# Loading the key weights in two transfers beside a second queue, with products of zeros ahead of the first folds

## The chip, the core and the metric

The kernel runs on one core of a Trainium2 chip. The core has five engines, each with its own instruction stream: TensorE (matrix products, PE in the profile, with its weight loads as PEld), VectorE (DVE), ScalarE (ACT), GpSimd (POOL) and SyncE (SP). SyncE only issues transfers here; SPq in the profile is its queue of issues. The engines wait for one another and for transfers by semaphores. The metric is the device time of one execution in microseconds (us); a run is told by its median over several executions. Beside the times there is one profiled execution, whose span runs from the first instruction to the last.

## What is computed

One block with a residual, over a sequence of 2048 positions with 512 channels. The input is layer-normalized; one branch is linear attention with a learned feature map, the other a gated two-layer network with a ReLU gate, whose output goes through SiLU and multiplies the attention's output.

```python
xn = layernorm(x)                                   # x: 2048 x 512
q, k, v = split(xn @ wqkv)                          # 32 heads of 16
pq, pk = q @ w_phi[h], k @ w_phi[h]                 # 16 x 16 per head
phi_q = concat(softmax(pq), softmax(-pq))
phi_k = concat(softmax(pk), softmax(-pk))
kv, z = phi_k.T @ v, sum(phi_k)
s = (phi_q @ kv / (phi_q @ z + 1e-6)) @ wo
gate, up = xn @ W_gate, xn @ W_up                   # 512 x 1376
g = silu(((gate * (gate > 0)) * up) @ W_down)
return x + s * g
```

All inputs and outputs are 32-bit floats.

## The kernel before

**Precision.** A 32-bit operand of a product is split into a high part, rounded to a format that TensorE multiplies in one pass (`F32R`), and a low part, the remainder. `split` (line 183) does this with one activation on ScalarE for the high part and one subtraction, on VectorE unless said otherwise, for the low part. `mm3` (line 188) then makes three products for each slice of 128 channels: low by high, high by low, high by high. So a projection of one tile of 128 positions is 12 products.

**The fold.** The feature map's weights `w_phi` are multiplied into the key and query weights once, at the start: `fold` (line 226) makes one slice of 128 rows of the combined weights by four plain 32-bit products of the raw weights (`wk_raw`, `wq_raw`, loaded transposed) with a block-diagonal constant `bd_sb` (tile `cb` in the profile, built on the host from `w_phi`). It returns a function that splits the result. There are four slices for keys and four for queries. Value weights are split without a fold (`wv_split`, line 852), with their low parts on GpSimd.

**The stages.** The 16 tiles of positions are normalized, transposed on TensorE by a product with an identity (`transpose_x`, line 277), split (`hi_xt`, `lo_xt`, lines 292 and 300, written to the tile `XT`), projected to keys, values and queries and turned into features; sums of key features with values are gathered in PSUM. Meanwhile the weights of the gated network are prepared. Then come two halves of that network with the queries' part of the attention beside it, and the output projection.

**Order.** The order of instructions on each engine is the order of the program's text (`InOrder`, line 39, keeps it), apart from work that a planner (`Clock`, line 56) inserts by estimated costs when it is pumped; the planner works while the program is built, with its own cost figures. An engine works through its instructions in order, and an instruction that waits holds back those behind it on its engine. On-chip buffers come from pools: `u2` has 44 buffers of 2 KB per partition, PSUM has 8 banks. Transfers from SyncE and ScalarE share eight semaphores in turn, so an issue waits until the transfer eight before it has landed.

**The start.** Lines 829 to 886 are the start of the program. SyncE issues x of the first tile, the block constants, the four slices of the key weights with the identity after the first slice, the second tile of x, halves of the query and value weights, and further tiles of x. `load_x` (line 213) issues one tile. VectorE computes the first tile's statistics and normalizes it (`norm_vector`, `norm_vector_apply`, lines 258 and 268), with GpSimd making the power of -1/2. TensorE's order is: folds of key slices 0 and 1, four transposes of the first tile (`turn`, line 304), folds of key slices 2 and 3, the 12 products of the first key projection (`pk`), folds of query slices 0 and 1, transposes of the second tile, folds of query slices 2 and 3, value projection (`pv`). The splits and `lo_xt` are in VectorE's order as the text has them: before the change the split of key slice 1 stands ahead of `lo_xt` of the first tile:

```python
    folds = [fold(WK, wk_raw[:, k, :], k) for k in range(2)]
    norm_vector_apply(0)
    folds[0]()
    px = turn(0, False)
    folds[1]()
    folds = [fold(WK, wk_raw[:, k, :], k) for k in range(2, KD)]
    lo_xt(*px)
    folds[0]()
    norm_vector(1)
    folds[1]()
    norm_vector_apply(1)
    pk = project(0, WK, "pk")
```

Nearly all instructions are recorded by one helper, so that the profile gives line 52 for them; tiles' names tell them apart: `pfold` is a fold's result, `pxT` a transposed tile, `wkh` and `wkl` the high and low part of a folded key slice, `wqh`, `wql` those of queries, `wvh`, `wvl` those of values, `xt` a tile of x, `xn` the normalized one.

Of the kernel before, what the change touches and what calls it, by code (L numbers as in the profile page):

```python
# [13 lines left out]
P = 128  # L14
# [5 lines left out]
KD = D // P  # L20
# [128 lines left out]
def layer_kernel(ctx: ExitStack, tc: tile.TileContext, x, wkT, wqT, wv, wo, wf, cst, out):  # L149
    pace = Clock()  # L150
    nc = InOrder(tc, pace)
# [4 lines left out]
    def ps(shape=(P, 512), name="ps"):  # L156
        return pp.tile(list(shape), F32, tag="ps", name=name)

    def u8(shape, name, dt=F32):
        return sb.tile(list(shape), dt, tag="u8", bufs=B8, name=name)  # L160
# [4 lines left out]
    def u2(shape, name, dt=F32):  # L165
        return sb.tile(list(shape), dt, tag="u2", bufs=B2, name=name)
# [7 lines left out]
    def f32(t):  # L174
        return t.bitcast(F32)

    def add(engine, o, a, b, op=ALU.add):
        engine.tensor_tensor(o, a, b, op=op)
# [31 lines left out]
    N = len(order)  # L210
    X = {}

    def load_x(n):
        b, i = order[n]
        t = b * TPB + i
        X[n] = u2((P, D), "xt")
        nc.sync.dma_start(X[n], x[t * P:(t + 1) * P, :])


    def w_tile(name):  # L220
# [5 lines left out]
    def fold(w, raw, k):  # L226

        p = ps(name="pfold")
        for j in range(KD):
            nc.tensor.matmul(p[:, j * P:(j + 1) * P], raw[:, j * P:(j + 1) * P], bd_sb[:, j, :],  # L230
                             start=True, stop=True)
        return lambda: split(*w[k], p)
# [44 lines left out]
    def transpose_x(n):  # L277
        p = ps((P, 2, 2, P), name="pxT")
        xn = XN.pop(n)
        for k in range(KD):  # L280
            transpose(p[:, k // 2, k % 2, :], xn[:, k * P:(k + 1) * P])
        return p

    def xt_parts(n, s):

        if n % 2 == 0:
            return [(XT[:, A11:A12 + 1, s, :, cols(n)], slice(0, 2))]
        if n not in A21:
            A21[n] = u2((P, 2, 2, P), "a21", F32R)
        return [(A21[n][:, s], 0), (XT[:, A22, s, :, cols(n)], 1)]  # L290

    def hi_xt(n, p):
        for to, c in xt_parts(n, 0):
            nc.scalar.activation(to, p[:, c], AF.Copy)

    def full_xt(n, p):
        XF[n] = u2((P, 2, 2, P), "xf")
        nc.scalar.activation(XF[n], p, AF.Copy)

    def lo_xt(n, p):  # L300
        for (to, c), (hi, _) in zip(xt_parts(n, 1), xt_parts(n, 0)):
            add(nc.vector, to, p[:, c], f32(hi), ALU.subtract)

    def turn(m, full=True):
        p = transpose_x(m)
        hi_xt(m, p)
        if full:
            full_xt(m, p)
        return m, p
# [519 lines left out]
    wk_raw, wv_raw, wq_raw = u8((P, KD, D), "wkT"), u8((P, KD, D), "wvr"), u8((P, KD, D), "wqT")  # L829
    bd_sb = u2((P, KD, P), "cb")  # L830
    ident = sb.tile([P, P], F32, name="ident")
    load_x(0)
    nc.sync.dma_start(bd_sb, cst[:, :KD, :])
    for k in range(KD):
        nc.sync.dma_start(wk_raw[:, k, :], wkT[:, k, :])
        if k == 0:
            nc.sync.dma_start(ident, cst[:, KD, :])
    load_x(1)
    nc.sync.dma_start(wq_raw[:, 0:2, :], wqT[:, 0:2, :])
    nc.sync.dma_start(wv_raw[:, 0:2, :], wv[:, 0:2, :])  # L840
    nc.sync.dma_start(wq_raw[:, 2:4, :], wqT[:, 2:4, :])
    load_x(2)
    nc.sync.dma_start(wv_raw[:, 2:4, :], wv[:, 2:4, :])
    for n in range(3, 7):
        load_x(n)
    mhalf = sb.tile([P, 1], F32, name="mhalf")
    nc.vector.memset(mhalf, -0.5)
    zacc = u4((P, H, 2, DH), "zacc")
# [7 lines left out]
    norm_vector_apply(0)  # L856
    folds[0]()
    px = turn(0, False)
    folds[1]()
    folds = [fold(WK, wk_raw[:, k, :], k) for k in range(2, KD)]  # L860
    lo_xt(*px)
    folds[0]()
    norm_vector(1)
    folds[1]()
# [9 lines left out]
    px = turn(1)  # L874
# [288 lines left out]
```

## Time and profile before

| what | value |
|---|---|
| median of 3 executions | 585.73 us (585.71 to 586.2) |
| profiled execution, its own time | 586.47 us |
| its span | 584.7 us |
| TensorE busy | 572.5 us (98%) |
| VectorE, ScalarE, GpSimd busy | 395.4, 288.6, 390.2 us |
| moved by transfers | 138.26 MB, 236 GB/s on average |

The span is shorter than the execution's own time by what lies around the first and last instruction. Rows of a timeline give the start in us from the span's start, the duration, the engine, the line, the operation, the tile written, the tiles read and how many instructions were merged; in brackets stands the idle time of the engine before it and what ended it. Rows of transfers give the size and the time from issue to landing. A plain 32-bit product of 128 by 128 with 128 columns appears as two instructions, here called passes.

### The profile page before, as it was taken

The numbers are of one execution on the slowest core, as the hardware profiler recorded it, in microseconds if no ns is written. First come the engines' busy times: TensorE is split into PE (matmuls) and PEld (weight loads), VectorE is DVE, ScalarE is ACT, GpSimd is POOL, SyncE is SP. The second block draws the span as 40 slices with busy tenths as digits, with TensorE's granted clock in tenths as the row PEclk, the third lists the DMA queues.
The fourth block names the chain that finished last, engine by engine and source line by source line (L and its number), as shares of the span: only waits on it lengthen the run. The fifth ranks groups of instructions, "written<-read, shape, count | busy, mean of one in ns | idle before, by whom it ended". The sixth has DMA issues, their size and how long they took to land.

```text
span 584.7 us, 8483 instructions
## 1 busy us (share of the span) xinstructions
PE 572.5 (98%) x2764; PEld 478.0 (82%) x2764; DVE 395.4 (68%) x604; ACT 288.6 (49%) x529; POOL 390.2 (67%) x341
## 2 busy tenths in 40 slices
PE   4999999999999999999999999999999999999997
PEld 4788888888888888888888888888888888888886
DVE  2898765876647976787784532488788868673323
ACT  3798786864635356245434151153554545534510
POOL 0669987998866576997967342544457585775394
PEclk9999999999999999999999999999999999999999
DMA  8358897974698938978967999995576475669863
GB/s 289 112 150 223 221 307 233 265 222 126 164 279 272 347 95 261 301 263 293 283 215 226 319 389 398 315 390 193 130 266 170 137 227 169 183 206 275 254 176 113
DMA packets 82844, 138.26 MB, mean 236 GB/s; under 512 B 7664, under 2 KB 30576, under 8 KB 81904
## 3 DMA queue, kind: packets, MB, share of 16 engines
q1 hardware_dynamic: 79488, 125.66, 64.3%
q0 software_dynamic: 3312, 12.06, 10.8%
q8 instruction: 22, 0.36, 0.3%
q14 instruction: 22, 0.18, 0.1%
HBM read 77.14 MB, written 52.69 MB: 222 GB/s over the span
## 4 chain that ended last, share of the span: by engine, by line
PE 97%; DMA 1%; ACT 1%; DVE 1%; SPq 0%; issue 0%; POOL 0%; POOLq 0%
PE py L52 21%; PE pd L52 10%; PE pa L52 10%; PE pc L52 10%; PE pso L52 8%; PE pk L52 8%; PE pq L52 7%; PE pv L52 7%; PE pb L52 5%; PE pkv L52 3%; PE pnum L52 3%; PE ppT L52 2%; PE pxT L52 1%; PE pfold L52 1%; DMA wkT<-wkT 1%; PE pkb L52 0%
## 5 line engine op out<-in xcount | busy, mean ns | idle before, releaser
L52 PE MATMUL pa<-XT,wa 128*128 128x512 f32 x264 | 68.9, 393 | 0.0
L52 PE MATMUL py<-fdh,hl 128*128 128x512 f32 x176 | 68.8, 391 | 0.0
L52 PE MATMUL py<-fdh,hh 128*128 128x512 f32 x176 | 68.6, 390 | 0.0
L52 PE MATMUL py<-fdl,hh 128*128 128x512 f32 x176 | 68.5, 389 | 0.0
L52 POOL TENSOR_TENSOR hl<-e,hh 128x512 fp32r<-128x512 f32 x22 | 28.4, 1292 | 56.5 <-ACT hh L52 56.2
L52 PEld LDWEIGHTS pa<-XT,wa 128*128 128x128 f32 x264 | 48.5, 188 | 9.4
L52 ACT ACTIVATE hh<-e 128x512 fp32r<-128x512 f32 x22 | 13.9, 632 | 72.1 <-DVE e L52 67.4
L52 POOL TENSOR_TENSOR phl<-ek,phl 128x1024 fp32r<-128x1024 f32 x15 | 36.1, 2403 | 17.9 <-ACT phl L52 17.9
L52 POOL TENSOR_TENSOR hl<-u,hh 128x512 fp32r<-128x512 f32 x22 | 28.5, 1296 | 27.1 <-ACT hh L52 24.8
L52 DVE TENSOR_TENSOR y<-py,y 128x512 f32<-128x512 f32 x40 | 27.5, 689 | 27.2 <-PE py L52 27.1
L52 POOL TENSOR_TENSOR y<-y,ys 128x512 f32<-128x512 f32 x24 | 31.1, 1297 | 17.0 <-ACT ys L52 17.0
L52 PEld LDWEIGHTS py<-fdh,hh 128*128 128x128 f32 x176 | 33.0, 188 | 7.0
L52 PEld LDWEIGHTS py<-fdl,hh 128*128 128x128 f32 x176 | 33.0, 188 | 6.7
L52 PEld LDWEIGHTS py<-fdh,hl 128*128 128x128 f32 x176 | 33.1, 188 | 6.7
L52 POOL TENSOR_TENSOR ez<-eq,zB 128x1024 f32<-128x1024 f32 x16 | 38.4, 2405 | 0.0
L52 DVE TENSOR_TENSOR pTl<-ppT,pTh 128x512 fp32r<-128x512 f32 x32 | 22.1, 690 | 23.1 <-ACT pTh L52 22.7
L52 PE MATMUL pd<-XT,wd 128*128 128x512 f32 x132 | 34.9, 395 | 0.0
L52 PE MATMUL pd<-XT,wc 128*128 128x512 f32 x132 | 34.5, 392 | 0.0
L52 PE MATMUL pb<-XT,wb 128*128 128x512 f32 x132 | 34.5, 393 | 0.0
L52 PE MATMUL pc<-XT,wb 128*128 128x512 f32 x132 | 34.3, 391 | 0.0
L52 POOL TENSOR_TENSOR ol<-of,oh 128x1024 fp32r<-128x1024 f32 x8 | 19.4, 2431 | 22.2 <-ACT oh L52 15.3
L52 PE MATMUL pc<-XT,wc 128*128 128x512 f32 x132 | 34.1, 391 | 0.0
(163 smaller groups left out, 1632.8 us busy)
## 6 DMA issues: line engine op xcount, KB each, us to landing
zacc<-ek POOLq DMA_DIRECT2D x15, 512.0 KB, 5.2
xts<-XT SPq DMA_DIRECT2D x4, 1792.0 KB, 11.3
XT<-xts SPq DMA_DIRECT2D x7, 1024.0 KB, 15.8
wa<-ws SPq DMA_DIRECT2D x26, 256.0 KB, 5.3
wb<-ws SPq DMA_DIRECT2D x26, 256.0 KB, 5.3
wc<-ws SPq DMA_DIRECT2D x26, 256.0 KB, 4.9
rawg<-wf SPq DMA_DIRECT2D x22, 256.0 KB, 3.9
ws<-wa SPq DMA_DIRECT2D x22, 256.0 KB, 3.9
```

Of the source, the lines that this page charges most:

```text
L52: return self.tc.keep_in_program_order(op(*a, **k))
```

## The change

The first tile of x, the block constants and the identity are issued by ScalarE, in this order, instead of SyncE. SyncE issues the key weights as two transfers of two slices each (512 KB), instead of four of 256 KB, and then goes on with the second tile of x and the other weights as before. A tile `idle` of 128 by 128 is set to zero by VectorE, and TensorE multiplies it with itself nine times into a PSUM tile that nothing reads. In the order of the program's text, `lo_xt` of the first tile now stands ahead of the split of key slice 1.

```diff
-    def load_x(n):
+    def load_x(n, queue=nc.sync):
         b, i = order[n]
         t = b * TPB + i
         X[n] = u2((P, D), "xt")
-        nc.sync.dma_start(X[n], x[t * P:(t + 1) * P, :])
+        queue.dma_start(X[n], x[t * P:(t + 1) * P, :])
...
-    load_x(0)
-    nc.sync.dma_start(bd_sb, cst[:, :KD, :])
-    for k in range(KD):
-        nc.sync.dma_start(wk_raw[:, k, :], wkT[:, k, :])
-        if k == 0:
-            nc.sync.dma_start(ident, cst[:, KD, :])
+    load_x(0, nc.scalar)
+    for k in (0, 2):
+        nc.sync.dma_start(wk_raw[:, k:k + 2, :], wkT[:, k:k + 2, :])
+    nc.scalar.dma_start(bd_sb, cst[:, :KD, :])
+    nc.scalar.dma_start(ident, cst[:, KD, :])
     load_x(1)
...
     for n in range(3, 7):
         load_x(n)
+
+    idle = u2((P, P), "idle")
+    nc.vector.memset(idle, 0.0)
+    p = ps((P, P), name="pidle")
+    for _ in range(9):
+        nc.tensor.matmul(p, idle, idle, start=True, stop=True)
     mhalf = sb.tile([P, 1], F32, name="mhalf")
...
     px = turn(0, False)
+    lo_xt(*px)
     folds[1]()
     folds = [fold(WK, wk_raw[:, k, :], k) for k in range(2, KD)]
-    lo_xt(*px)
     folds[0]()
```

## The prediction

> **What bounds the kernel now.** The page comes first: its span, its slices and the chain that ended last.
>
> ```profile
> span 584.7 us, 8483 instructions
> ...
> PE   4999999999999999999999999999999999999997
> ...
> PE 97%; DMA 1%; ACT 1%; DVE 1%; SPq 0%; issue 0%; POOL 0%; POOLq 0%
> ```
>
> TensorE is the bound: full in every slice but the first and the last, and 97% of the chain. Time can be had only where TensorE stands still, or runs slowly. The second view is the list of waits for TensorE over the whole run (us in total, times, longest).
>
> ```profile
> PE pfold L52 <- DMA wkT<-wkT: 7.1, 1, 7.1
> PE pk L52 <- DVE XT L52: 0.8, 1, 0.8
> PE pv L52 <- POOL wvl L52: 0.5, 2, 0.3
> PE pxT L52 <- DVE lr L52: 0.2, 1, 0.2
> ```
>
> The change touches the first two rows alone: 7.1 us until the key weights have landed, and 0.8 us before the first key projection. After them TensorE has almost no idle time, so what is won here reaches the end of the run unless a later wait takes it back. The third view is the timeline of the start (start and duration in us; SPq is SyncE's queue of issues).
>
> ```profile
> 0.75 1.28 ACT L52 ACT_TABLE_LOAD   x1 [0.75 <-PEq L1155]
> 0.75 0.38 SPq L52 DMA_DIRECT2D xt<-x  x1
> 0.82 0.06 DVE L52 MEMSET mhalf<- 128x1 f32 x1 [0.82 <-PEq L1155]
> 1.18 0.42 SPq L52 DMA_DIRECT2D cb<-cst  x1
> 1.65 0.42 SPq L52 DMA_DIRECT2D wkT<-wkT  x1
> ...
> 2.60 1.38 SPq L52 DMA_DIRECT2D wkT<-wkT  x3
> 3.49 0.69 DVE L52 BATCH_NORM_STATS2 bs<-xt 128x6 f32<-128x512 f32 x1 [2.61 <-DMA xt<-x]
> ...
> 4.49 0.43 SPq L52 DMA_DIRECT2D wqT<-wqT  x1
> ...
> 4.97 0.58 SPq L52 DMA_DIRECT2D wvr<-wv  x1
> 5.26 0.55 DVE L52 TENSOR_SCALAR xn<-xt,bm,br 128x512 f32<-128x512 f32 x1 [0.68 <-POOL br L52]
> ...
> 7.06 3.75 PE L52 MATMUL pfold<-cb,wkT 128*128 128x128 f32 x16 [7.06 <-DMA wkT<-wkT]
> ...
> 10.60 1.05 PE L52 MATMUL pxT<-ident,xn 128*128 128x128 f32 x4
> ...
> 11.46 1.99 PE L52 MATMUL pfold<-cb,wkT 128*128 128x128 f32 x16
> 11.70 0.60 ACT L52 ACTIVATE XT<-pxT 128x512 fp32r<-128x512 f32 x1 [1.96 <-PE pxT L52]
> ...
> 12.81 0.69 DVE L52 TENSOR_TENSOR wkl<-pfold,wkh 128x512 fp32r<-128x512 f32 x1 [2.35 <-ACT wkh L52]
> 13.42 0.68 DVE L52 TENSOR_TENSOR XT<-pxT,XT 128x512 fp32r<-128x512 f32 x1
> ...
> 14.02 0.68 DVE L52 TENSOR_TENSOR wkl<-pfold,wkh 128x512 fp32r<-128x512 f32 x1
> ...
> 14.25 0.47 PE L52 MATMUL pk<-wkh,XT 128*128 128x512 f32 x1 [0.81 <-DVE XT L52]
> ...
> 14.62 0.69 DVE L52 BATCH_NORM_STATS2 bs<-xt 128x6 f32<-128x512 f32 x1
> ...
> 15.62 0.68 DVE L52 TENSOR_TENSOR wkl<-pfold,wkh 128x512 fp32r<-128x512 f32 x1
> ...
> 16.64 0.39 PE L52 MATMUL pk<-wkl,XT 128*128 128x512 f32 x1
> ...
> 17.10 1.95 PE L52 MATMUL pfold<-cb,wqT 128*128 128x128 f32 x16
> ...
> 18.88 0.60 PE L52 MATMUL pxT<-ident,xn 128*128 128x128 f32 x4
> ...
> 19.32 1.95 PE L52 MATMUL pfold<-cb,wqT 128*128 128x128 f32 x16
> ```
>
> A fold of two key tiles is 16 passes. From the start of one group to the next, the first such pair takes 10.60 - 7.06 = 3.54 us, the same shape later 18.88 - 17.10 = 1.78 us; four transposes take 11.46 - 10.60 = 0.86 us at first and 19.32 - 18.88 = 0.44 us later. So TensorE runs at half rate from its first instruction until about 11.46, 4.40 us later.
>
> The fourth view is that of the transfers, one issue at a time (KB each, us from issue to landing), with the rate of the first 32 us in slices of 0.8 us.
>
> ```profile
> GB/s 0 0 113 379 256 145 250 231 243 289 333 417 422 425 407 425 397 422 397 392 389 361 254 18 0 20 0 0 0 0 0 0 0 133 195 0 0 0 54 338
> ...
> xt<-x SPq DMA_DIRECT2D x1, 256.0 KB, 2.7
> cb<-cst SPq DMA_DIRECT2D x1, 256.0 KB, 2.9
> wkT<-wkT SPq DMA_DIRECT2D x1, 256.0 KB, 5.3
> wkT<-wkT SPq DMA_DIRECT2D x1, 256.0 KB, 5.2
> wkT<-wkT SPq DMA_DIRECT2D x1, 256.0 KB, 6.2
> wqT<-wqT SPq DMA_DIRECT2D x1, 512.0 KB, 7.2
> wvr<-wv SPq DMA_DIRECT2D x1, 512.0 KB, 8.0
> ```
>
> With the issues above, x lands at 3.45, the constants at 4.08, the first key tile at 6.95, the second at 7.80, the fourth (issued near 3.55) at 9.75. While the key tiles move, in rows of 2 KB, the rate falls to 145 to 250 GB/s. The half query and half value weights, 512 KB in rows of 4 KB, land at 11.69 and 12.97, 1.28 us apart (410 GB/s).
>
> **The change part by part.** *Transfers.* SyncE issues two key transfers of 512 KB, in 4 KB rows, at once; ScalarE issues x, the block constants and the identity, at about 0.43 us each, and then loads its table (1.28 us), done near 0.75 + 1.3 + 1.28 = 3.3, long before its first activation. The first fold now waits for the constants and for both first key tiles. Were bytes alike whatever their order, x, constants and two key tiles would still land at 7.80, and the fold start near 7.9: that is the late end. If 4 KB rows move at the 410 GB/s of the query and value halves and the two queues share equally, 512 KB of keys are added to what landed by 4.08: 4.08 + 1.28 + 0.1 to start = 5.46. If SyncE's queue gets two bytes for ScalarE's one, the constants have another 512 KB ahead of them: 6.74. No row shows two such queues at once. I take 5.8, nearer to equal shares since the rows of 410 GB/s have the new keys' shape. The second pair of keys is needed 2.2 us after the first, which 1.28 us covers; the identity (64 KB behind the constants) is needed 1.8 us after. With no x ahead of its chain but keys beside it, x may land 0.6 us later, its normalized tile at about 6.4 instead of 5.8; the transposes want it at 7.6.
>
> The Trainium skill, "DMA: Bandwidth & Descriptors", section "Issuing engines are not separate DMA queues", speaks against this part: both queues end in the same 16 DMA engines, and a second issuing engine saves only the time of issuing. By it alone the fold would start near 7.9 and the sum below would be 2.1 us smaller.
>
> *Products of zeros.* VectorE's memset of 128 x 128 is no row; it lies between 0.06 us (128 x 1) and the 0.55 us of a 128 x 512 operation, I take 0.2. TensorE then starts at about 1.15. Nine products are 18 passes at 3.54 / 16 = 0.22 us: busy until 5.1, in idle time. If weights landed before that, the fold would wait for the zeros, so 5.1 is the early end of its start. Full rate came 4.40 us after the first pass in the trace; 1.15 + 4.40 = 5.55, before the fold's 5.8. So the first pair takes 1.78 instead of 3.54 and the transposes 0.44 instead of 0.86: 2.18 us. If the clock doesn't come up, this is lost.
>
> The Trainium skill, "TensorE: Matmul & The Clock Gate", section "What's actually happening", has a free-running activity window of about 3.4 us; 4.40 us fits that. By it full rate comes 3.4 to 6.8 us after the zeros begin, an estimate of 4.6 to 8.0.
>
> *The low half of x before the second key split.* The second pair of folds begins at 11.46 and, at 1.78, is through at 13.24, yet the projection starts at 14.25 because VectorE does the second key split (12.81) ahead of x's low half (13.42). With the order turned, x's low half can follow the activation (0.60) directly: transposes at 7.58, activation at 7.58 + 0.64, low half 8.85 to 9.55, products free to begin at 9.7. TensorE's own folds end at 5.8 + 1.78 + 0.44 + 1.78 = 9.80. So that wait, 14.25 - 13.24 = 1.01 us, goes. Next late is the fourth key split: VectorE now does low half, two splits (0.6 us each from start to start), statistics, then the fourth split 1.00 us after these (15.62 - 14.62): 8.85 + 1.8 + 1.0 = 11.65, ending 12.35; its product is due at 9.80 + (16.64 - 14.25) = 12.19. Waiting behind it on TensorE are the rest of that projection and the query folds: +0.2 us.
>
> *Sum.* 7.06 to 5.8: -1.26; clock -2.18; wait -1.01; new wait +0.2: -4.25 us. Everything after moves along: query weights (landed 11.69 already before) are needed at 12.85, and the value weights at 12.97, by the faster order near 10, are read by ScalarE from about 10.5. The span goes from 584.7 to 580.45. The profiled execution took 586.47, 0.74 over the median of 585.73; against the median, **581.5 us**.
>
> **Rivals.** *The clock isn't up when the folds come.* The pause after the zeros (5.1 to 5.8) may restart the count, or zeros may not count. Then the fold pair and transposes run at half rate: the start and the order remain, 1.26 + 1.01 - 0.2 = 2.1 us, between nothing and all of the 2.18 lost: 581.5 to 583.7, about 583.3 as a typical case. For it: no row shows such a pause, or operands of zeros. Against: the pause is short, and in the trace the 4.40 us ran on through folds and transposes alike.
>
> *The queues bring nothing.* Fold start at 7.9 with full clock: +0.84 - 2.18 - 1.01 + 0.2 = -2.15 us, 583.6. For it: the same bytes. Against: 410 against 145 to 250 GB/s.
>
> *Given back.* Something later is late: the value splits on GpSimd already hold TensorE (0.5 us in the list of waits). They follow on work that moves along, so this is weak; about 585.5.
>
> *Slower.* SyncE issues five transfers without waiting for any (two of keys, x, half query, half value: 2.25 MB). If its queue is served first, the constants follow all of these. At 410 GB/s from about 1.6 us that is near 9; TensorE has then stood for 4 us and is at half rate again. With half rate for the pair and transposes the projection starts at 9 + 3.54 + 0.86 + 1.78 = 15.2, and later clock adds some: 1 to 2 us slower, 587.1. It decides once constants land later than about 8.0 at half rate (14.25 - 6.18), or 10.2 at full rate. Against: before, one queue was served in order and nothing shows a preference.
>
> **Chances.** Main case 0.55 (its own range 580.6 to 582.4: fold between 5.1 and 6.7); clock 0.17; queues 0.14; given back 0.08; slower 0.06. The range reaches over the first three: 580.5 to 584.5. A measurement tells about 0.2%, 1.17 us, from no change. Faster by more: 0.55 + 0.17 + 0.13 = 0.85; within: 0.09; slower: 0.06.
>
> **What would show it.** Right: products of zeros from about 1.15 to 5.1; first fold at 5.1 to 6.7, released by constants or keys; a pair at 1.8 us; first projection at about 9.8 and no wait on x's low half, a short one on the fourth split; the query folds at about 12.85 instead of 17.10, and the same lead at 40 us and at the end. Wrong: a pair at 3.5 us (clock), a fold at 7 or later (queues), or a lead that shrinks after 13 us (given back).

## The result and the profile after

The changed kernel is slower: a median of 587.26 us against 586.16 us before (14 executions each), a ratio of 1.0021 with a 95% interval of 1.0013 to 1.0028. A gain of 4.25 us was forecast; 1.1 us were lost. The profiled execution took 587.43 us, its span 585.7 us.

The list of waits for TensorE (us in total, times, longest) in the changed kernel:

```profile
PE pfold L52 <- DMA cb<-cst: 3.1, 1, 3.1
PE pidle L52 <- DVE mhalf L52: 1.1, 1, 1.1
PE pv L52 <- POOL wvl L52: 0.5, 2, 0.3
PE pxT L52 <- DVE lr L52: 0.2, 1, 0.2
```

The wait on x's low half is gone, as forecast. The first fold no longer waits for keys but for the block constants, and does so after the products of zeros are over. The transfers of the changed kernel, one issue at a time (KB, us from issue to landing), and the rate of the first 32 us in slices of 0.8 us:

```profile
GB/s 0 0 92 274 264 277 399 410 396 417 421 410 415 402 394 420 394 387 384 382 346 82 0 0 0 20 0 0 0 0 0 0 0 0 97 230 0 0 0 95
...
wkT<-wkT SPq DMA_DIRECT2D x1, 512.0 KB, 5.3
xt<-x ACTq DMA_DIRECT2D x1, 256.0 KB, 5.4
wkT<-wkT SPq DMA_DIRECT2D x1, 512.0 KB, 6.7
cb<-cst ACTq DMA_DIRECT2D x1, 256.0 KB, 7.0
```

The issues stand at 0.74, 0.74, about 1.2 and 1.18. So x lands at 6.1 (before: 3.45) together with the first half of the keys, and the constants at 8.2 (before: 4.08), after the second half of the keys (7.9). The timeline of the start in the changed kernel:

```profile
0.74 0.41 ACTq L52 DMA_DIRECT2D xt<-x  x1
0.74 0.86 SPq L52 DMA_DIRECT2D wkT<-wkT  x2
0.84 0.17 DVE L52 MEMSET idle<- 128x128 f32 x1 [0.84 <-PEq L1160]
...
1.06 4.21 PE L52 MATMUL pidle<-idle 128*128 128x128 f32 x18 [1.06 <-DVE mhalf L52]
1.18 0.46 ACTq L52 DMA_DIRECT2D cb<-cst  x1
...
8.34 3.75 PE L52 MATMUL pfold<-cb,wkT 128*128 128x128 f32 x16 [3.07 <-DMA cb<-cst]
...
11.88 1.06 PE L52 MATMUL pxT<-ident,xn 128*128 128x128 f32 x4
...
12.74 2.52 PE L52 MATMUL pfold<-cb,wkT 128*128 128x128 f32 x16
...
15.01 0.48 PE L52 MATMUL pk<-wkh,XT 128*128 128x512 f32 x1
...
17.38 0.19 PEld L52 LDWEIGHTS pk<-wkl,XT 128*128 128x128 f32 x1 [0.24 <-DVE wkl L52]
...
17.95 1.95 PE L52 MATMUL pfold<-cb,wqT 128*128 128x128 f32 x16
```

The first fold starts 1.28 us later than before (8.34 against 7.06). The first pair of folds takes 11.88 - 8.34 = 3.54 us, exactly as before, so the zeros did nothing for it; the second pair is partly slow too (15.01 - 12.74 = 2.27 us against 1.78), because full rate came only at 13.93, the first change in the trace's record of the clock. The projection starts 0.76 us late, the query folds 0.85 us late, and it stays like that: the last product of the output starts at 581.68 instead of 580.87.

### The profile page after: what moved, and what is told of

Its sections match the earlier page's. It is cut to its first block, busy times and chain, and to the rows that moved or that the text cites. A ratio compares the mean times of both kernels' runs of the same rounds, so it can differ in the third digit from the quotient of the medians.

```text
span 585.7 us, 8515 instructions
## 1 busy us (share of the span) xinstructions
PE 577.1 (99%) x2782; PEld 482.7 (82%) x2782; DVE 395.8 (68%) x605; ACT 288.8 (49%) x529; POOL 390.0 (67%) x341
## 4 chain that ended last, share of the span: by engine, by line
PE 97%; DMA 1%; ACT 1%; DVE 1%; POOL 0%; issue 0%; ACTq 0%; POOLq 0%
PE py L52 20%; PE pd L52 10%; PE pa L52 10%; PE pc L52 10%; PE pso L52 8%; PE pk L52 8%; PE pq L52 7%; PE pv L52 7%; PE pb L52 5%; PE pkv L52 3%; PE pnum L52 3%; PE ppT L52 2%; PE pfold L52 1%; DMA cb<-cst 1%; PE pxT L52 1%; PE pkb L52 0%
```

## Experiments

Theory after the result: two things went wrong in turn. The constants, issued beside the keys instead of ahead of them, shared the transfer engines with them and came late; and the zeros, over by 5.3, could not keep the clock up until 8.3. The rivals: the loss comes from the zeros themselves, zeros don't count for the clock at all, or the turned order only moves the wait. Ratios below are against the kernel before, with 95% intervals.

### The transfers alone

The changed kernel without zeros and with the old order of `lo_xt`; the rest of the change stays. Against the changed kernel:

```diff
-    idle = u2((P, P), "idle")
-    ... (memset and nine products)
     px = turn(0, False)
-    lo_xt(*px)
     folds[1]()
     folds = [fold(WK, wk_raw[:, k, :], k) for k in range(2, KD)]
+    lo_xt(*px)
```

> The new transfers alone: keys in two pieces on SyncE, x, constants and identity on ScalarE; no products of zeros, the old order of the low half of x. Theory A (the loss of the change comes from the transfers): the constants land near 8.2 us again, the first fold starts near 8.3 at half rate instead of 7.06, and the kernel is slower than before by 1.3 us or a little more, more than the whole change, since the turned order is missing. Theory B (the loss comes from the products of zeros): the constants land before 7 and the kernel is no slower than before.

587.79 us, ratio 1.0032 (1.002 to 1.0044): 1.7 us slower by the medians, more than the whole change. The fold waits for the same tile, until nearly the same time. The timeline:

```profile
8.23 3.75 PE L52 MATMUL pfold<-cb,wkT 128*128 128x128 f32 x16 [8.23 <-DMA cb<-cst]
```

So the loss lies in the transfers (theory A), not in the zeros.

### The zeros alone

```diff
+    idle = u2((P, P), "idle")
+    nc.vector.memset(idle, 0.0)
+    p = ps((P, P), name="pidle")
+    for _ in range(9):
+        nc.tensor.matmul(p, idle, idle, start=True, stop=True)
     mhalf = sb.tile([P, 1], F32, name="mhalf")
```

> The kernel before with the nine products of zeros alone. They end near 5.3, the fold starts at 7.06 after a pause of 1.8 us. If products of zeros count for the clock and a short pause doesn't matter: the first pair of folds takes 1.8 us instead of 3.5, and about 2 us are won. If a pause of 1.8 us loses what was gathered, or zeros don't count: the pair takes 3.5 us and the time is that of before within 0.3 us.

585.51 us, ratio 0.999 (0.998 to 1.0): 0.6 us faster by the medians, at the edge of the noise, and well short of the 2 us of the first forecast. This profile (585.82 us) shows what happened in one execution. The view of windows (from and to, length, busy time of TensorE, its weight loads, VectorE, ScalarE and GpSimd, then the granted clock, share of transfers, GB/s):

```profile
1.36:4.77 3.41, 3.41 (x17) 3.41 (x17) 1.03 (x3) 0.66 (x1) 0.18 (x1) 1.00 0.71 204
4.77:8.18 3.41, 1.24 (x11) 1.08 (x10) 0.55 (x1) 0.00 (x0) 0.38 (x1) 1.00 0.85 261
8.18:11.60 3.42, 3.42 (x18) 3.42 (x18) 0.69 (x1) 1.14 (x3) 0.00 (x0) 0.50 1.03 411
11.60:14.00 2.40, 1.93 (x16) 1.73 (x15) 1.82 (x4) 1.97 (x5) 0.00 (x0) 1.00 1.03 414
```

The clock changed at 4.77, 8.19 and 11.60, 3.41 us apart each time. After a stretch full of zeros it rose; after a stretch with TensorE busy for 1.24 of 3.41 us it fell, in the middle of the folds; after a full stretch of folds and transposes it rose again. (Ahead of the first change on record the view prints 1.00 where the passes run at half rate, as in its first row; there the rate must be read from the passes.) So zeros count for the clock, as folds do. This agrees with the free-running window of about 3.4 us in the Trainium skill, "TensorE: Matmul & The Clock Gate", section "What's actually happening". The eleven executions differ: three, the profiled one among them, have a mean granted clock of 0.997 (one stretch of 3.41 us at half rate after a first rise takes 3.41 x 0.5 / 584, or 0.003, off the mean) and took 585.35 to 586.32 us; three others took 584.09 to 584.40 us, near the 2 us that the first forecast had.

### The order alone

```diff
     px = turn(0, False)
+    lo_xt(*px)
     folds[1]()
     folds = [fold(WK, wk_raw[:, k, :], k) for k in range(2, KD)]
-    lo_xt(*px)
```

> The kernel before with the low half of x ahead of the second key split, and nothing else. By the prediction's step: the wait of 0.8 us ahead of the first key projection goes, and at most 0.2 us come back before the fourth low product: faster by 0.6 to 1.0 us. The rival, that the wait only moves to the fourth split: no gain.

585.01 us, ratio 0.9983 (0.9975 to 0.9992): 1.1 us faster by the medians. The list of waits has no row for x's low half:

```profile
PE pfold L52 <- DMA wkT<-wkT: 6.6, 1, 6.6
PE pv L52 <- POOL wvl L52: 0.5, 2, 0.3
PE pxT L52 <- DVE lr L52: 0.2, 1, 0.2
```

The first row shows too that the landing of the keys moves between executions (6.6 here, 7.1 in the profile before), so the start of one profile is not the median's. The clock, too, rose earlier in this profile (10.19 us, before 11.52), so the gain is read from the medians, not from the two profiles.

### Fourteen products of zeros

As the zeros alone, with `range(14)`.

> The kernel before with fourteen products of zeros, which reach from 1.05 to about 7.05, so that TensorE has no pause before the first fold. If products of zeros count for the clock: full rate at the first fold, pair 1.8 us, transposes 0.45, and 2 us won against before. If they don't count: the pair takes 3.5 us, full rate comes 4.4 us after the first fold or later, and nothing is won; the fold may start up to 0.2 us late.

584.52 us, ratio 0.9974 (0.9964 to 0.9984): 1.6 us faster, of the 2 us forecast. In its timeline the first pair runs at full rate, and so do the transposes:

```profile
1.06 4.75 PE L52 MATMUL pidle<-idle 128*128 128x128 f32 x28 [1.06 <-DVE mhalf L52]
6.88 2.03 PE L52 MATMUL pfold<-cb,wkT 128*128 128x128 f32 x16 [1.06 <-DMA wkT<-wkT]
8.75 0.60 PE L52 MATMUL pxT<-ident,xn 128*128 128x128 f32 x4
9.18 1.95 PE L52 MATMUL pfold<-cb,wkT 128*128 128x128 f32 x16
```

The zeros were expected to last until 7.05 and did not: full rate came at 3.95, and the rest of them ran twice as fast. A pause of 1.06 us remained and the clock stayed up through it.

### The changed kernel with more zeros

The changed kernel with `range(24)`.

> The changed kernel with 24 products of zeros instead of nine, so that TensorE is busy from 1.05 to between 7.8 and 9.4 us. Theory: the nine products failed because their 4.2 us gave no whole window of activity and the pause to the late constants was 3.1 us. Then full rate comes near 4 to 7.5 us, the first pair of folds takes 1.8 us from about 8.3 on, and the kernel gets 2 to 2.5 us faster than the changed one, so about 1 us faster than before. Rival: the clock is lost for another reason; then the pair takes 3.5 us still and nothing is won.

586.52 us, ratio 1.0016 (1.0002 to 1.003), with executions from 585.16 to 589.83 us. The profile (585.97 us) has the first pair from 9.26 to 11.04, at full rate, so the clock rose as expected. But the kernel is still slower than before, and the gain over the changed kernel is 0.7 us by the medians, not clear of the noise, instead of 2 to 2.5. In this execution full rate came at 6.83, the 48 passes ended after 9, and the fold waited for them, though the constants had landed at 8.3; that the slowest executions are those where it came later still is argued, not shown. A fixed number of products is a stretch of time only once it is known when the clock rises.

### Keys in 2 KB rows beside the second queue

The transfers alone, with SyncE's two key transfers made four:

```diff
-    for k in (0, 2):
-        nc.sync.dma_start(wk_raw[:, k:k + 2, :], wkT[:, k:k + 2, :])
+    for k in range(KD):
+        nc.sync.dma_start(wk_raw[:, k, :], wkT[:, k, :])
```

> The transfers of the change alone, but with the key weights in four transfers of 256 KB (2 KB rows) on SyncE; no zeros, old order. Theory: the two queues take turns piece by piece, so that 4 KB rows got two bytes for one. With 2 KB rows on both sides x lands with the first key tile and the constants with the second; at 250 to 400 GB/s x lands near 4.5 to 5 and the constants near 6 to 7.5 us, more than 0.7 us before the 8.2 us of the run with two pieces. Rival, that SyncE's queue is simply preferred or ScalarE's is slow: x at 6 or later and the constants at 8 or later, as with two pieces.

586.76 us, ratio 1.0018 (1.001 to 1.0027). The transfers (issued at about 0.75, 0.75 and 1.2):

```profile
xt<-x ACTq DMA_DIRECT2D x1, 256.0 KB, 5.0
wkT<-wkT SPq DMA_DIRECT2D x1, 256.0 KB, 4.8
...
cb<-cst ACTq DMA_DIRECT2D x1, 256.0 KB, 6.6
wkT<-wkT SPq DMA_DIRECT2D x1, 256.0 KB, 6.1
```

Again x lands with the first key transfer, though that is now half as large, and the constants come just after the second. What each queue had moved by 6.1 us (packets, MB, share of the engines' time; q1 is SyncE's queue, q10 ScalarE's), first in the changed kernel, then here:

```profile
q1 hardware_dynamic: 235, 0.90, 45.0%
q10 hardware_dynamic: 192, 0.36, 18.9%
```

```profile
q1 hardware_dynamic: 307, 0.58, 38.6%
q10 hardware_dynamic: 241, 0.44, 20.8%
```

The bytes stood at 2.5 to 1 with 4 KB rows and at 1.3 to 1 with 2 KB rows, the packets at 1.2 and 1.3 to 1. That fits queues that take turns packet by packet, and not a preferred SyncE queue. But the constants came only 0.3 us earlier than in the transfers alone (7.8 against 8.1), less than the 0.7 expected, as the engines moved less as well: 1.02 MB by 6.1 us against 1.26. So the ratio of bytes is a part of the delay. That the larger part is the sharing with the first key rows, while these are slow, is argued from these times and not shown by a run of its own.

### Keys in two transfers on one queue

```diff
-    for k in range(KD):
-        nc.sync.dma_start(wk_raw[:, k, :], wkT[:, k, :])
+    for k in (0, 2):
+        nc.sync.dma_start(wk_raw[:, k:k + 2, :], wkT[:, k:k + 2, :])
         if k == 0:
             nc.sync.dma_start(ident, cst[:, KD, :])
```

> The kernel before with the key weights in two transfers of 512 KB, all on SyncE's queue in the old order (x, constants, keys 0 and 1, identity, keys 2 and 3); no zeros, old order of splits. If 4 KB rows move at 410 GB/s from the start: constants at 4.1, keys 0 and 1 at about 5.4, fold at 5.5 and 1.5 us won. If the first key rows are slow whatever their length, as the 280 GB/s between 2.5 and 4.5 us of the changed kernel suggest: keys at 6 to 7, fold within 1 us of 7.06, and a gain of 0 to 1 us.

586.48 us, ratio 1.0014 (1.0005 to 1.0023): slower, which neither expectation had. Its profile is of its fastest execution (586.06 us):

```profile
wkT<-wkT SPq DMA_DIRECT2D x1, 512.0 KB, 5.0
```

The keys land at 1.67 + 5.0 = 6.7, 2.55 us after the constants at 4.1. For their 512 KB alone that is 206 GB/s; with what moved beside them the engines moved 0.78 MB in that time, 300 GB/s, and not 410. So 4 KB rows don't cure the slow stretch. That the kernel got slower because the first fold now waits for two key tiles instead of one is the likely reason, argued and not shown.

### One queue, two key transfers, order and fourteen zeros

The edits of the last, the third and the fourth run together.

> One queue in the old order with keys in two transfers, fourteen products of zeros, and the low half of x ahead of the second key split. If the parts add: about 1.1 us from the order, 1.6 from the zeros and 0 to 1 from the transfers, so 2.7 to 3.7 us faster than before; the first key projection at 10.5 to 11.3 us. If the fourth key split now holds the projection, 0.2 to 0.4 us less.

584.93 us, ratio 0.9986 (0.9974 to 0.9998), 1.0 us faster instead of 2.7 to 3.7. In the profile the fold starts at 8.16 at full rate, after a pause of 2.25 us. The two key tiles landed 6.4 us after their issue at 1.66, in the same arrangement that took 5.0 us in the run before. So the landing of the first keys spreads by over a us between executions, and waiting for two tiles has no gain to show for it. Late keys can cost the clock as well: three of the twelve executions have a mean granted clock of 0.997 and took 586.71 to 586.88 us, the other nine (0.999 or 1.0) 583.55 to 585.31.

### Order and fourteen zeros, transfers untouched

> The kernel before, its transfers untouched, with the low half of x ahead of the second key split and fourteen products of zeros. If the two parts add: 1.0 us from the order and 1.6 from the zeros, 583.3 to 583.6 against 586, ratio near 0.9957. If the key weights' transfers were needed too, or the fourth key split takes back a part, the ratio stays at 0.997 or above.

583.47 us (5 executions, 583.16 to 583.82), ratio 0.9952 (0.9939 to 0.9966): 2.6 us faster than before and 3.8 us faster than the changed kernel. The two parts add up (1.1 + 1.6) within the noise. Its timeline:

```profile
1.06 5.91 PE L52 MATMUL pidle<-idle 128*128 128x128 f32 x28 [1.06 <-DVE mhalf L52]
...
7.10 2.02 PE L52 MATMUL pfold<-cb,wkT 128*128 128x128 f32 x16
...
8.96 0.60 PE L52 MATMUL pxT<-ident,xn 128*128 128x128 f32 x4
...
9.40 1.95 PE L52 MATMUL pfold<-cb,wkT 128*128 128x128 f32 x16
...
11.10 0.48 PE L52 MATMUL pk<-wkh,XT 128*128 128x512 f32 x1
```

The first projection starts at 11.10, 3.15 us before that of the old profile. This version beats both kernels.

### Query weights ahead of the keys

One issue moved in the kernel before: the first half of the query weights goes between the constants and the keys.

> The kernel before with one issue moved: the first half of the query weights (512 KB, 4 KB rows) ahead of the key weights. It tells what makes the keys slow. If it is the key weights' own place in memory or their row length: the query half lands 1.3 us after the constants, near 5.4, and the keys keep their slow pieces after that. If it is the time since the start: the query half is as slow as the keys were (2.5 us or more after the constants, at 6.6 or later), and the keys behind it move at near 390 GB/s, 0.7 us apart. The kernel itself gets 1 to 3 us slower either way.

587.85 us in a single execution, so only its profile is read here. The transfers, issued at 1.19, 1.66 and 2.12, and the rate of the first 12 us in slices of 0.3 us:

```profile
GB/s 0 0 0 0 0 27 123 14 348 396 396 423 458 410 314 355 130 96 55 75 109 114 118 155 166 234 326 355 410 389 369 444 417 396 417 437 444 437 382 396
...
cb<-cst SPq DMA_DIRECT2D x1, 256.0 KB, 3.0
wqT<-wqT SPq DMA_DIRECT2D x1, 512.0 KB, 4.6
...
wkT<-wkT SPq DMA_DIRECT2D x1, 256.0 KB, 6.7
```

The query half moved at 314 to 458 GB/s from 3.6 to 4.8, and the rate then fell to 55 to 166 until about 7.5; the query half landed at 6.26, the first key tile at 8.8. This is neither clean outcome: the query rows were fast at a time when the keys had been slow before, and their last part was caught in a slow stretch of its own. The stretch starts when the first keys are read, in this run as before (where the rate fell after the constants) and in the changed kernel (slow from its first slices to 4.8, fast from then on). What makes these first reads slow stays open.

### The changed kernel without its zeros

> The changed kernel without its nine products of zeros: transfers and order stay. If zeros that end 3.1 us before the fold are worth nothing: the same time as the changed kernel within 0.3 us, that is 1.0 to 1.3 us slower than before, although transfers (1.7 slower) and order (1.1 faster) measured alone add up to 0.6 slower. If the zeros help in some phases of the clock: 0.3 us or more slower than the changed kernel, 1.4 us or more slower than before.

587.2 us, ratio 1.0021 (1.0012 to 1.0029), the same as the changed kernel. Nine zeros that end three us ahead of the fold are worth nothing there by the median. Transfers and order measured alone add up to 0.6 us slower, not 1.2; the intervals of the two allow either.

## Why the prediction was wrong

**The start of the first fold** (-1.26 us, measured +1.28) is the step that failed. I let the second queue do no harm: between equal shares (5.46) and two to one (6.74), with 7.9 as the late end if rows stayed slow. Two things came together that I had bounded one at a time. The shares were such that all the keys landed ahead of the constants, and the keys' first rows stayed slow: 274, 264 and 277 GB/s from 2.4 us on, 399 only from 4.8. The 410 GB/s was taken from query and value rows that move later; in the run with one queue the same 4 KB key rows took 2.55 us for 512 KB, with the engines at 300 GB/s. And the late end of 7.9 counted x, constants and half the keys, while by 8.2 the other half had gone too. What the transfers had moved by 8.2 us, before and after the change:

```profile
DMA packets 968, 1.58 MB, mean 193 GB/s; under 512 B 99, under 2 KB 227, under 8 KB 968
```

```profile
DMA packets 901, 2.11 MB, mean 257 GB/s; under 512 B 89, under 2 KB 210, under 8 KB 901
```

So more had been moved than before, not less, but the constants, which the first fold needs, came late among it. Two unknowns that multiply need the product of their ends. The rule of the Trainium skill, "DMA: Bandwidth & Descriptors", section "Issuing engines are not separate DMA queues", that a second issuing engine only saves issue time, was nearer than my sum, which had set it aside (7.9 by it, 8.34 measured). x, too, came 2.7 us later than before instead of 0.6; that cost nothing, because the late fold put its transposes off to 11.88.

**The clock** (-2.18; in the profile 0, and 0.49 lost in the second pair) failed too. That zeros raise the clock was right (five runs), but 4.40 us after the first product is not a delay: it was the place of the window's border in one execution. Stepping back by 3.41 us from the change at 13.93, the windows of the changed kernel are:

```profile
0.28:3.69 3.41, 2.63 (x12) 2.63 (x13) 0.17 (x2) 1.28 (x1) 0.17 (x4) 1.00 0.44 123
3.69:7.10 3.41, 1.58 (x8) 1.28 (x6) 0.86 (x2) 0.00 (x0) 0.00 (x0) 1.00 1.00 361
7.10:10.51 3.41, 2.17 (x10) 2.20 (x11) 0.72 (x3) 0.09 (x1) 0.56 (x1) 1.00 1.06 417
10.51:13.93 3.42, 3.42 (x18) 3.42 (x18) 1.01 (x2) 1.46 (x3) 0.00 (x0) 1.00 1.02 398
```

TensorE was busy for 77%, 46% and 64% of the first three, and only the full fourth raised the clock. This is the profiled execution, and not all were like it. Nine of its fourteen executions have a mean granted clock of 0.997 or 0.993, where no execution of a kernel without zeros on record has less than 0.998: in these nine the zeros seem to have raised the clock, and it fell again before the folds were through, as in the profile of the zeros alone. The six with 0.997 took 586.20 to 587.32 us, the three with 0.993 587.52 to 587.76 and the other five 587.06 to 587.43, so at best a part of the 2.18 us was won. The rival that the clock isn't up was right in kind, and its chance (0.17) too low: nine products (4.2 us) are barely longer than a window (3.41 us) whose place is not known, and the late constants left a pause of 3.07 us behind them.

**x's low half** (-1.01) held: the wait is gone, and alone it was worth 1.1 us. **The fourth key split** (+0.2) came as forecast but smaller: the weight load waits 0.24 us for it, and TensorE's lag grows by 0.09 us, from 0.76 at the projection to 0.85 at the query folds. **What follows** held: nothing was given back or won after 18 us. The terms as measured, 1.28 + 0.49 - 1.01 = 0.76, are the lag of the first projection.

**The slower rival** had the right place and price (587.1 us; decided when constants land after 8.0 at half rate; they landed at 8.2) but the wrong cause: SyncE's queue was not served first; both went on side by side, with 2.5 bytes to one by 6.1 us. I gave it 0.06 because one queue in order had shown no preference, which says nothing of two.

## What to carry to other kernels

What the first product waits for should stand first on the queue, alone: what is put on a second queue beside it shares the engines with everything else. Here the transfers moved more by 8.2 us than before, and the constants still landed 4.1 us later. Idle time ahead of the first product can be used to raise TensorE's clock, but by filling it up to the real work or close to it (a pause of 1.06 us did no harm; after one near 2.2 us the clock was lost in one profile and held in another), since the clock goes by stretches of activity whose borders move from run to run. Measure the order of two small operations apart from such edits, as here the one sure gain (1.1 us) was hidden in a change that lost.

## What was not expected of the hardware

In these traces the clock needed less than a full stretch to rise, and held through a partly idle one. Stretches of 3.41 us ending at a change of clock or in step with one: it rose after 2.89 us busy (85%, fourteen zeros) and 3.11 us (91%, one queue with all), not after 2.63 (77%, changed kernel) or 2.36 (69%, 24 zeros). It stayed up after 2.35 us (69%, fourteen zeros) and 1.75 us (51%, one queue with all), and fell after 1.24 (36%, nine zeros). The windows of these, fourteen zeros first and then one queue with all:

```profile
0.54:3.95 3.41, 2.89 (x13) 2.89 (x14) 0.51 (x3) 1.28 (x1) 0.00 (x0) 1.00 0.50 180
3.95:7.36 3.41, 2.35 (x21) 2.19 (x20) 1.24 (x4) 0.00 (x0) 0.56 (x1) 1.00 0.79 207
```

```profile
0.76:4.17 3.41, 3.11 (x14) 3.11 (x15) 0.88 (x4) 1.26 (x1) 0.00 (x0) 1.00 0.60 189
4.17:7.59 3.42, 1.75 (x16) 1.55 (x14) 0.87 (x3) 0.00 (x0) 0.56 (x1) 1.00 0.83 232
```

While the first key weights were read, all transfers together ran far below the some 410 GB/s seen later, for 2.4 to 4.5 us, in 2 KB and in 4 KB rows: at 116 to 300 GB/s in the kernel before, 239 to 314 with the keys in two transfers on one queue, 55 to 166 with query weights first (slices of 0.3 us). What moved beside them was slow as well. Why is not known.
